# Unread f32 matmuls in TensorE's waits, and another split of the output projection, in a one-core decode kernel

## The chip, the cores and the metric

The kernel runs on one core of a Trainium2 chip. The metric is the device time of one execution in microseconds (us); the time of a kernel is the median of several executions. A profile is of one execution, and names the engines PE (TensorE matmuls), PEld (TensorE weight loads), DVE (VectorE), ACT (ScalarE), POOL (GpSimd) and SP (SyncE, which here only issues and awaits DMAs).

## What is computed

One decode step for two sequences (B = 2, one query each, D = 448), in bf16:

```python
xn = layernorm(A_x)                                  # 2 x 1 x 448
q  = (xn @ wq).reshape(B, 1, 16, 256)                # 16 query heads of 256
k, v = k_cache[:, :, -2048:], v_cache[:, :, -2048:]  # 8 key heads, each for two query heads
p  = softmax(q . k * 256**-0.5)
s  = (p . v).reshape(B, 1, 4096) @ wo                # wo: 4096 x 448
g  = silu(relu(xn @ w1) @ w2)                        # 448 -> 1792 -> 448
out = A_x + s * g
```

All matmuls have two tokens (or two tokens by two heads) of rows, so nearly all of the work is reading the caches and the weights once: 44.11 MB.

## The kernel before

**Loads.** All large loads are issued by SP in one queue, in program order: wq in two parts, K of turn 0, K of turn 1, V of turn 0, and later K and V of the following turns, w1 and w2 (L572, L573), V of the last turn (L588) and wo in pieces (L590 to L593). A turn is one quarter of the (sequence, key head) pairs; there are `NQ` = 4. K has two buffers, V one; wo goes into the first K buffer (L266). The next load of V waits for the PV that last read the buffer, the load of K for the DVE transposes that read it, and wo for the transposes of turn 2. SP takes its list in order, so each wait also holds what stands behind it.

**A turn.** DVE transposes K into `kt` (`do_T`, L455), PE makes the scores in `sbk` (`do_S`, L463, the two halves SA and SB), DVE takes the maxima, PE and DVE bring them to a bias (`ch_rmT`, `ch_mrow`, `ch_exp`), ACT takes the exponentials, DVE transposes them into `pt`. PE multiplies by V into `obk`, 32 matmuls on four column tiles (`do_PV`, L479); ACT scales the result to `o_sb` (L488); PE transposes that into `nbk` with four small matmuls (`do_oT`, L491, section OT), and DVE masks it into `at_exp` (`do_at`, L529).

**The order on PE.** PE's instructions are written into sections that `_Prog.run` (L115) lays out as a program with branches: SA, SB, PV, OT and CH are bodies that all turns share, with the turn in a register, so what stands in OT once runs in each of the four turns. The prologue (PRO), FFN, WO and END run once. PE takes its instructions in order, and each waits only for the operations named in its list of dependencies.

**The end.** With all turns but the last PV done, PE runs the FFN (`do_H`, `do_F`, L410 to L436), then PV, OT of the last turn. In WO two small matmuls fold `at_exp` (L609 to L612), DVE casts the result to `at2` (L613). wo has 32 rows per partition, of 448 columns each. The first `WO_WIDE` rows are "wide" (L615 to L619): one matmul of 448 columns a row, four rows side by side on the four column tiles of the array, row j on tile j % 4, summed into four places of `wbk`. DVE copies `wbk` to `wsum` (L620), and four f32 matmuls with `sel` add the four places into `cbk`, where the output's 448 columns lie as four tiles of 112 (L631 to L635). The rows left are "narrow" (`narrow`, L622): four matmuls of 112 columns a row, side by side, that add into the same places of `cbk`. Section END begins with the first row of the last piece of wo (L637). Then DVE multiplies by the gate and adds x (L640, L642), and ACT issues the DMA of the output.

wo comes in pieces of `WO_PARTS` rows (L194), each with a semaphore of its own; the first row of each piece waits for it. Before, these are 18, 8, 4 and 2 rows, with 26 wide ones (L195), so the wide rows end with the second piece.

`ident_f` is a 128 x 128 identity in f32 in SBUF. `sbk`, `obk`, `wbk`, `cbk` and so on are banks of PSUM, 128 x 512 in f32.

Of the kernel before, what the change touches and what calls it, by code (L numbers as in the profile page):

```python
# [11 lines left out]
PE, DVE, ACTE, SP, POOL = "pe", "dve", "act", "sp", "pool"  # L12
# [153 lines left out]
def bass_recurrent_scan__sliding_block_cached__dense_activation_relu__decode_kernel(  # L166
# [24 lines left out]
    SLOTS = 7  # L191
    HC = HD // 2
    FC = DFF // 2
    WO_PARTS = [18, 8, 4, 2]  # L194
    WO_WIDE = 26  # L195
    NCOL = D // 4
    QW = 24 + 8 * 128
    BIG = 1e30
# [2 lines left out]
    with es:  # L201
        pr = _Prog(nc, es)

        def named(name, shape, dt):
            return es.enter_context(nc.sbuf_tensor(name, shape, dt))

        def psum(name, shape, dt):
            return es.enter_context(nc.psum_tensor(name, shape, dt))

        def view(t, off, dims, n=128, p0=0, pstep=1):  # L210
            width = t.shape[1]
            return bass.AP(t, p0 * width + off, [[width * pstep, n]] + dims)

        ident = named("ident", [128, 128], BF)
        ident_f = named("ident_f", [128, 128], F32)
# [52 lines left out]
        sbk = psum("sbk", [128, 512], F32)  # L268
        obk = psum("obk", [128, 512], F32)
        fbk = psum("fbk", [128, 512], F32)  # L270
        wbk = psum("wbk", [128, 512], F32)
# [109 lines left out]
        def mm(out_ap, lhsT, rhs, start, stop=False, **kw):  # L381
            return lambda e: e.matmul(out_ap, lhsT=lhsT, rhs=rhs, start=start, stop=stop,  # L382
                                      skip_group_check=True, **kw)
# [95 lines left out]
        def do_PV(k):  # L479
            deps = [d_v[k], st["pt", k]]  # L480
            for n in range(NT // 2):
# [6 lines left out]
            st["osb", k] = pr.op(ACTE, lambda e: e.activation(  # L488
                o_sb[:, :], obk[:, :], ACT.Copy, scale=rs[:, k:k + 1]), [st["PV", k], st["rs", k]], key="osb")

        def do_oT(k):  # L491
            pr.section("OT", k + 1)
            deps = [st["osb", k]]
            for dhi in range(2):
                for t2 in range(2):
                    lo = 256 * t2 + 128 * dhi
                    o = pr.op(PE, mm(view(nbk, dhi, [[2, 8]]), o_sb[:, lo:lo + 128],
                                     fold[:, 8 * t2:8 * t2 + 8], dhi == 0 and t2 == 0, dhi == 1 and t2 == 1), deps)
                    deps = []
            st["oT", k] = o  # L500
# [57 lines left out]
        for k in range(1, NQ):  # L558
            if k > 1:
                ch_max(k)  # L560
            pr.section("PV", k)
            do_PV(k - 1)
            if k == 1:
                do_S(1, 1)
                ch_max(1)
            do_oT(k - 1)
            do_at(k - 1)
            load_v(k) if k < 3 else None
            if k == 1:
                load_k(3)  # L570
            if k == 2:
                d_w1 = pr.dma(SP, wbuf[:, 0:W2], w1_src, [st["q_mm"]])  # L572
                d_w2 = pr.dma(SP, wbuf[:, W2:W2 + 14 * D], w2_src)  # L573
            pr.section("CH", k)
            ch_rmT(k)
            ch_mrow(k)
            ch_exp(k)
            early = 2 if k == 1 else 0
            for e in range(early):
                do_T(k + 1, e)  # L580
            ch_pt(k)
            if k + 1 < NQ:
                do_qbd(k + 1)
                for e in range(early, 8):
                    do_T(k + 1, e)
                do_S(k + 1, 0)
                do_S(k + 1, 1)
        load_v(3)  # L588
        landed, j0 = {}, 0
        for n in WO_PARTS:  # L590
            landed[j0] = pr.dma(SP, wo_sb[:, j0 * D:(j0 + n) * D], wo_src[:, j0 * D:(j0 + n) * D],
# [10 lines left out]
        pr.section("PV", NQ)  # L602
        do_PV(NQ - 1)
        do_oT(NQ - 1)
        do_at(NQ - 1)

        pr.section("WO", 0)
        deps = [st["at", NQ - 1]]
        for b in range(2):  # L609
            m_at = pr.op(PE, mm(mbk[:, 256 + 32 * b:288 + 32 * b], at_exp[:, 128 * b:128 * b + 128],  # L610
                                fold[:, :], b == 0, b == 1), deps)
            deps = []  # L612
        v_at2 = pr.op(DVE, lambda e: e.tensor_copy(at2[:, :], mbk[:, 256:320]), [m_at])  # L613
        deps = [v_at2]
        for j in range(WO_WIDE):  # L615
            i = j % 4
            m_w = pr.op(PE, mm(wbk[32 * i:32 * i + 2, 0:D], view(at2, j, [[32, 2]]), wo_sb[:, j * D:(j + 1) * D],
                               j < 4, j + 4 >= WO_WIDE, tile_position=(0, 32 * i)), deps + [landed.get(j)])
            deps = []  # L619
        v_ws = pr.op(DVE, lambda e: e.tensor_copy(wsum[:, :], wbk[:, 0:D]), [m_w])  # L620

        def narrow(j):  # L622
# [9 lines left out]
        for i in range(4):  # L632
            pr.op(PE, mm(cbk[32 * i:32 * i + 17, 0:NCOL], sel[:, :], wsum[:, i * NCOL:(i + 1) * NCOL],
                         True, tile_position=(0, 32 * i)), deps)
            deps = []  # L635
        for j in range(WO_WIDE, 32):
            if j == max(landed):  # L637
# [39 lines left out]
```

## Time and profile before

| | |
|---|---|
| three executions, us | 110.31, 110.70, 110.76 |
| median | 110.7 us |
| the profiled execution's own time | 110.01 us |
| its span, first to last instruction | 108.7 us |
| mean granted TensorE clock in it | 0.874 |
| PE, DVE, ACT, POOL busy | 65.5, 62.2, 14.9, 7.9 us |
| DMA queue of the large loads | 44.11 MB, 95.1% of 16 engines' span |

The profile's times are microseconds from the span's start. A line of the timeline gives start, length, engine, line of the kernel, operation, written tile <- read tiles, shapes and count; the brackets hold the idle time of the engine before it and what ended it. Most matmuls have the line of a helper, L382, so they are told apart by their tiles. `kbuf` with `in_A_wo` as its source is wo, since wo lies in the first K buffer. `at` is `at2`. A row of the windows view gives a stretch, its length, busy us and instructions of PE, PEld, DVE, ACT and POOL, the granted TensorE clock (1.00 is full speed), the share of the DMA engines and GB/s. The chain that ended last is followed back from the last instruction, at each step to what released it.

### The profile page before, as it was taken

What the parts mean: (1) busy time and instruction counts of PE and PEld (TensorE: products, weight loads), DVE (VectorE), ACT (ScalarE), POOL (GpSimd) and SP (SyncE); (2) the same over time, 40 slices, a digit from 0 to 9 for tenths busy, and PEclk for the clock granted to TensorE, in tenths of its full rate; (3) what the DMA queues carried; (4) which work ended last, traced back from release to release, by engine and by line L of the source; (5) the groups of instructions that cost most, each with busy time, mean ns of one, the idle gap of its engine ahead of it and who ended that gap; (6) DMA issues with size and microseconds to landing.
All of it is one profiled execution on the core that took longest, in us unless ns stands there. A gap on an engine that the chain in (4) does not pass through costs nothing.

```text
span 108.7 us, 1107 instructions
## 1 busy us (share of the span) xinstructions
PE 65.5 (60%) x412; PEld 25.2 (23%) x412; DVE 62.2 (57%) x106; ACT 14.9 (14%) x33; POOL 7.9 (7%) x31
## 2 busy tenths in 40 slices
PE   0000930069973999942899954079994596675561
PEld 0000200023422333421334312024331331322210
DVE  1689078199948999043999413299932226214022
ACT  2991000000003001103000023000002300054000
POOL 6500023000021000030000210000000000000000
PEclk9999999999999759998559999557999556999769
DMA  3999998999899989998999889998999989999960
GB/s 72 457 423 448 458 458 386 434 446 470 386 422 410 519 386 422 398 531 386 398 422 531 386 386 434 458 458 386 404 415 402 539 386 422 410 435 392 417 239 1
DMA packets 2332, 44.11 MB, mean 406 GB/s; under 512 B 282, under 2 KB 412, under 8 KB 668
## 3 DMA queue, kind: packets, MB, share of 16 engines
q1 hardware_dynamic: 2304, 44.11, 95.1%
q10 hardware_dynamic: 28, 0.01, 0.0%
HBM read 44.11 MB, written 0.00 MB: 406 GB/s over the span
## 4 chain that ended last, share of the span: by engine, by line
DMA 61%; PE 20%; DVE 12%; SPq 2%; issue 1%; ACT 1%; DVEq 0%; ACTq 0%
DMA kbuf<-in_A_k_cache_dram 42%; DMA kbuf<-in_A_wo_dram 19%; PE sbk L382 14%; DVE kt L460 10%; PE obk L382 3%; SPq L46 2%; PE wbk L382 1%; ACT e_sb L521 1%; PE cbk L382 1%; DVE rm L503 1%; DVE wsum L620 1%; PE mbk L382 0%; PE nbk L382 0%; DVE mx L512 0%; DVE tmp L640 0%
## 5 line engine op out<-in xcount | busy, mean ns | idle before, releaser
L382 PE MATMUL sbk<-kt,qbd 128*128 128x512 bf16 x128 | 36.5, 449 | 13.1 <-DVE kt L460 13.0
L460 DVE STREAM_TRANSPOSE kt<-kbuf 128x1024 f32<-128x1024 f32 x32 | 36.7, 1206 | 7.2 <-DMA kbuf<-in_A_k_cache_dram 7.2
L382 PEld LDWEIGHTS sbk<-kt,qbd 128*128 128x128 bf16 x128 | 13.6, 110 | 35.3 <-issue 23.8
L382 PE MATMUL fbk<-wbuf,xq 128*4 128x512 bf16 x28 | 3.2, 627 | 10.9 <-DVE xq L369 10.9
L405 POOL COPY qbd<-qt 32x64 bf16<-32x64 bf16 x16 | 4.5, 284 | 54.1 <-PE sbk L382 42.2
L382 PE MATMUL obk<-vbuf,pt 128*16 128x512 bf16 x128 | 7.6, 379 | 0.8 <-DMA vbuf<-in_A_v_cache_dram 0.8
L488 ACT ACTIVATE o_sb<-obk,rs 128x512 bf16<-128x512 f32 x4 | 2.8, 688 | 37.7 <-PE obk L382 37.1
L503 DVE TENSOR_REDUCE rm<-sbk 128x1 f32<-128x512 f32 x4 | 2.8, 692 | 7.5 <-PE sbk L382 4.0
L520 ACT ACTIVATE bias<-mbk 128x1 f32<-128x1 f32 x4 | 0.7, 171 | 33.7 <-PE mbk L382 33.7
L526 DVE STREAM_TRANSPOSE pt<-e_sb 128x512 bf16<-128x512 bf16 x4 | 2.7, 687 | 3.2 <-ACT e_sb L521 3.2
L382 PE MATMUL nbk<-ssum,gsum 128*128 128x1 f32 x8 | 1.7, 286 | 4.5 <-ACT e_sb L521 4.5
L530 DVE TENSOR_TENSOR at_exp<-nbk,qmask 128x64 bf16<-128x64 f32 x4 | 0.9, 222 | 5.7 <-PE nbk L382 5.7
L382 PEld LDWEIGHTS obk<-vbuf,pt 128*16 128x16 bf16 x128 | 2.8, 89 | 5.3 <-DMA vbuf<-in_A_v_cache_dram 1.7
L382 PE MATMUL fbk<-wbuf,h_sb 128*17 128x448 bf16 x14 | 2.8, 352 | 2.0 <-DVE h_sb L426 2.0
L382 PE MATMUL wbk<-kbuf,at 128*2 128x448 bf16 x26 | 2.9, 565 | 1.5 <-DMA kbuf<-in_A_wo_dram 1.4
L382 PEld LDWEIGHTS fbk<-wbuf,xq 128*4 128x4 bf16 x28 | 0.8, 108 | 12.4 <-issue 11.8
L382 PE MATMUL mbk<-one_f,mrow 1*128 1x1 f32 x8 | 1.5, 256 | 2.8 <-DVE mrow L515 2.8
L620 DVE COPY wsum<-wbk 128x448 f32<-128x448 f32 x1 | 0.6, 624 | 4.2 <-PE wbk L382 4.2
L359 DVE TENSOR_SCALAR xg<-x_sb,st,rstd 2x384 bf16<-2x384 bf16 (+2 forms) x5 | 2.9, 601 | 0.1
L382 PE MATMUL cbk<-wbuf,xr 128*4 128x448 bf16 x7 | 2.8, 577 | 0.0
L521 ACT ACTIVATE e_sb<-sbk,bias 128x512 bf16<-128x512 f32 x4 | 2.7, 687 | 0.4
L382 PE MATMUL fbk<-wbuf,xr 128*4 128x448 bf16 x7 | 2.8, 571 | 0.0
(81 smaller groups left out, 43.7 us busy)
## 6 DMA issues: line engine op xcount, KB each, us to landing
kbuf<-in_A_k_cache_dram SPq DMA_DIRECT2D x4, 4096.0 KB, 23.1
vbuf<-in_A_v_cache_dram SPq DMA_DIRECT2D x4, 4096.0 KB
wbuf<-in_B_w_dram SPq DMA_DIRECT2D x2, 1568.0 KB, 20.8
wbuf<-in_A_wq_dram SPq DMA_DIRECT2D x1, 2560.0 KB, 10.4
kbuf<-in_A_wo_dram SPq DMA_DIRECT2D x1, 2016.0 KB, 19.0
wbuf<-in_A_wq_dram SPq DMA_DIRECT2D x1, 1024.0 KB, 4.8
kbuf<-in_A_wo_dram SPq DMA_DIRECT2D x1, 896.0 KB, 20.6
kbuf<-in_A_wo_dram SPq DMA_DIRECT2D x1, 448.0 KB, 21.3
```

The source lines that it names most:

```text
L46: o = _Op(eng, lambda e: e.dma_start(dst, src), deps, True, key)
L359: xs["xn"] = pr.op(DVE, lambda e: e.tensor_scalar(out=view(xg, 128 + 128 * lo + shift, [[256, blocks], [128, 2], [pairs, 128 // pairs]], n=B),
L382: return lambda e: e.matmul(out_ap, lhsT=lhsT, rhs=rhs, start=start, stop=stop, skip_group_check=True, **kw)
L405: st["qbd", k] = pr.op(POOL, lambda e, a=a: e.tensor_copy(view(qbd, 24 + 32 * a, [[128, 8], [2, 4], [1, 2]], n=32, p0=32 * a), view(qt, 0, ...
L460: st["T", k, e] = pr.op(DVE, lambda e: e.transpose(view(dst, lo, [[128, NT // 2], [1, 32]]), view(src, lo, [[128, NT // 2], [1, 32]])), de ...
L488: st["osb", k] = pr.op(ACTE, lambda e: e.activation(o_sb[:, :], obk[:, :], ACT.Copy, scale=rs[:, k:k + 1]), [st["PV", k], st["rs", k]], ke ...
L503: st["rm", k] = pr.op(DVE, lambda e: e.tensor_reduce(out=rm[:, :], in_=sbk[:, :], axis=AX.X, op=ALU.max), [st["S", k, 7]], key="rm")
L520: a = pr.op(ACTE, lambda e: e.activation(bias[:, :], mbk[:, 128:129], ACT.Copy), [o])
L521: st["exp", k] = pr.op(ACTE, lambda e: e.activation(e_sb[:, :], sbk[:, :], ACT.Exp, bias=bias[:, 0:1], accum_out=ssum[:, 0:1]), [a], key=" ...
L526: st["pt", k] = pr.op(DVE, lambda e: e.transpose(pt[:, :], e_sb[:, :]), [st["exp", k]], key="pt")
L530: st["at", k] = pr.op(DVE, lambda e: e.tensor_tensor(out=view(at_exp, 16 * k, [[64, 4], [4, 4], [1, 4]]), in0=view(nbk, 0, [[4, 4], [1, 4] ...
L620: v_ws = pr.op(DVE, lambda e: e.tensor_copy(wsum[:, :], wbk[:, 0:D]), [m_w])
```

## The change

wo's pieces become 18, 6, 6 and 2 rows, and 24 rows are wide instead of 26; the wide rows still end with the second piece, and six rows instead of four come between them and the last piece. A new helper puts a matmul on PE that multiplies the f32 identity by itself, repeated to n columns, into a bank that nobody reads at that time. It depends on nothing and nothing depends on it. It stands

- at the head of OT, ahead of the matmuls that wait for `o_sb`, in all four turns: 256 columns into `wbk`;
- in WO behind the two folding matmuls: 512 columns into `sbk`;
- behind wide row 17, the last of the first piece: 384 columns into `sbk`;
- behind the last wide row, 23: 256 columns into `sbk`.

```diff
-    WO_PARTS = [18, 8, 4, 2]
-    WO_WIDE = 26
+    WO_PARTS = [18, 6, 6, 2]
+    WO_WIDE = 24
...
+        def keep_busy(bank, n):
+            pr.op(PE, lambda e: e.matmul(bank[:, 0:n], lhsT=ident_f[:, :],
+                                         rhs=view(ident_f, 0, [[0, n // 128], [1, 128]]), start=True, stop=True))
+
         def do_oT(k):
             pr.section("OT", k + 1)
+            keep_busy(wbk, 256)
             deps = [st["osb", k]]
...
             deps = []
+        keep_busy(sbk, 512)
         v_at2 = pr.op(DVE, lambda e: e.tensor_copy(at2[:, :], mbk[:, 256:320]), [m_at])
         deps = [v_at2]
         for j in range(WO_WIDE):
...
             deps = []
+            if j == WO_PARTS[0] - 1:
+                keep_busy(sbk, 384)
+            if j == WO_WIDE - 1:
+                keep_busy(sbk, 256)
         v_ws = pr.op(DVE, lambda e: e.tensor_copy(wsum[:, :], wbk[:, 0:D]), [m_w])
```

## Prediction

> **What bounds the kernel now.** I read the page's slices and its chain first, then the DMA issues, then the chain in order of time, and last the end of the timeline beside the granted clock. The page:
>
> ```profile
> span 108.7 us, 1107 instructions
> ...
> DMA  3999998999899989998999889998999989999960
> ...
> HBM read 44.11 MB, written 0.00 MB: 406 GB/s over the span
> ...
> DMA 61%; PE 20%; DVE 12%; SPq 2%; issue 1%; ACT 1%; DVEq 0%; ACTq 0%
> ...
> kbuf<-in_A_wo_dram SPq DMA_DIRECT2D x1, 2016.0 KB, 19.0
> kbuf<-in_A_wo_dram SPq DMA_DIRECT2D x1, 896.0 KB, 20.6
> kbuf<-in_A_wo_dram SPq DMA_DIRECT2D x1, 448.0 KB, 21.3
> kbuf<-in_A_wo_dram SPq DMA_DIRECT2D x1, 224.0 KB, 21.4
> ```
>
> The DMA row is full from the second slice to the last but two: the kernel streams 44.11 MB, and nothing that TensorE does earlier moves the last byte as long as the queue keeps work. It does: the last V load, 4.19 MB, is issued at 82.14 and is landed when its PV starts at 96.98 (row below); at 406 GB/s it takes 10.3, so it began at 86.7 and had stood in line for some 4.5 us, with the wo pieces behind it. So only the end counts, behind the wo pieces. The chain in order of time, and the issues:
>
> ```profile
> 82.14 0.55 SPq L46
> ...
> 82.73 0.59 SPq L46
> ...
> 83.36 20.61 DMA kbuf<-in_A_wo_dram
> ...
> 104.02 0.95 PE wbk L382 x5
> ...
> 104.99 0.64 DVE wsum L620
> ...
> 105.66 0.70 PE cbk L382 x32
> ...
> 106.39 0.28 DVE tmp L640
> ...
> 106.70 0.28 DVE out_sb L642
> ```
>
> ```profile
> L46 SPq DMA_DIRECT2D kbuf<-in_A_wo_dram x4: 432/432/591, 82.7 to 84.3; - x4
> ```
>
> The pieces are issued at 82.73, 83.36, 83.83 and 84.31 (591 ns, then 432 ns each, about 0.04 between). With the page's times to landing they are there at 101.73, 103.97, 105.13 and 105.71. The chain follows the second piece: eight wide rows (0.95), the copy to wsum (0.64), then 8 sel and 24 narrow matmuls (0.70), and two VectorE operations. The last piece, at 105.71, lands just as sel starts at 105.66, so it isn't what ended last, but it is next in line.
>
> The clock comes from the windows view, cut where the grant changes. The changes lie on a grid of 3.41 us; the columns are length, PE busy, and further on PEclk:
>
> ```profile
> 81.31:84.72 3.41, 1.55 (x23) 0.65 (x15) 0.63 (x3) 0.88 (x3) 0.00 (x0) 1.00 0.99 416
> 84.72:88.13 3.41, 2.60 (x8) 1.22 (x9) 0.77 (x2) 0.76 (x2) 0.00 (x0) 0.50 1.23 525
> 88.13:91.55 3.42, 3.30 (x9) 0.89 (x7) 1.77 (x5) 0.00 (x0) 0.00 (x0) 0.50 0.93 402
> 91.55:94.96 3.41, 1.58 (x9) 0.82 (x10) 1.61 (x4) 0.00 (x0) 0.00 (x0) 1.00 0.94 404
> 94.96:98.37 3.41, 2.62 (x35) 1.08 (x37) 1.03 (x2) 2.02 (x8) 0.00 (x0) 1.00 1.01 432
> 98.37:101.78 3.41, 0.99 (x18) 0.29 (x10) 0.77 (x4) 0.69 (x1) 0.00 (x0) 1.00 0.91 385
> 101.78:105.20 3.42, 2.95 (x26) 0.66 (x26) 0.21 (x1) 0.00 (x0) 0.00 (x0) 0.50 0.94 373
> 105.20:108.61 3.41, 0.68 (x32) 0.52 (x32) 0.96 (x3) 0.00 (x0) 0.00 (x0) 1.00 0.00 1
> ```
>
> Each window's work sets the next window's clock. In 91.55:94.96, 1.58 us of long matmuls (46%) keep it at full; in 98.37:101.78, 0.99 (29%) halves it. The 1.55 of 81.31:84.72 halves it too, but half of that is short matmuls of 1 to 128 columns, mostly latency; its long ones, the PV of 80.19, end at 82.09, 0.78 us or 23%. So I count long ones, and the bound to hold full clock lies between about 29% and 46%. To come back, 61% (2.09 us of 84.72:88.13, from 86.04) was not enough and 86% was. The wide rows ran at half clock, and in this execution the grid was kind: the clock came back at 105.20, just ahead of sel.
>
> **The change part by part.** The rows that price it:
>
> ```profile
> 80.19 1.90 PE L382 MATMUL obk<-vbuf,pt 128*16 128x512 bf16 x32
> ...
> 86.04 2.77 PE L382 MATMUL fbk<-wbuf,xr 128*4 128x448 bf16 x7
> ...
> 88.61 2.82 PE L382 MATMUL cbk<-wbuf,xr 128*4 128x448 bf16 x7
> ...
> 93.38 2.81 PE L382 MATMUL fbk<-wbuf,h_sb 128*17 128x448 bf16 x14 [1.95 <-DVE h_sb L426]
> ...
> 96.98 1.90 PE L382 MATMUL obk<-vbuf,pt 128*16 128x512 bf16 x32 [0.79 <-DMA vbuf<-in_A_v_cache_dram]
> ...
> 98.99 0.69 ACT L488 ACTIVATE o_sb<-obk,rs 128x512 bf16<-128x512 f32 x1 [0.64 <-issue]
> 99.73 0.17 PEld L382 LDWEIGHTS nbk<-fold,o_sb 128*128 128x128 bf16 x4 [1.34 <-ACT o_sb L488]
> ...
> 100.31 0.21 PE L382 MATMUL mbk<-fold,at_exp 128*128 128x32 bf16 x2 [0.32 <-DVE at_exp L530]
> 100.56 0.23 DVE L613 CAST at<-mbk 128x64 bf16<-128x64 f32 x1 [0.31 <-PE mbk L382]
> ...
> 101.89 3.04 PE L382 MATMUL wbk<-kbuf,at 128*2 128x448 bf16 x26 [1.37 <-DMA kbuf<-in_A_wo_dram]
> ...
> 105.66 0.39 PE L382 MATMUL cbk<-wsum,sel 128*17 128x112 f32 x8 [0.73 <-DVE wsum L620]
> ...
> 105.87 0.48 PE L382 MATMUL cbk<-kbuf,at 128*17 128x112 bf16 x24
> ```
>
> ```profile
> 84.02 0.29 PEld L382 LDWEIGHTS mbk<-one_f,mrow 1*128 1x128 f32 x2 [0.89 <-DVE mrow L515]
> ...
> 85.53 0.50 PEld L382 LDWEIGHTS nbk<-ssum,gsum 128*128 128x128 f32 x2 [1.22 <-ACT e_sb L521]
> ```
>
> *One f32 filler.* No long f32 matmul stands in the trace. The four sel calls are eight instructions, so one f32 call is two. They occupy 105.66 to 105.87, 0.21 us for 112 columns on four tiles side by side. The 24 narrow bf16 matmuls, six rounds of 112 columns, take 0.48 less the last one's 0.21, so 0.045 a round. One f32 call thus costs about 0.21/0.045 = 4.6 bf16 rounds, latency included; I take 4, the count near it without latency. By the 14 rows of 93.38 (2.81 us, 0.19 a row of 448 columns) a bf16 column costs 0.42 ns at full clock; at half clock 0.82 (88.61 less 86.04 over 7 rows). Fillers of 256, 384 and 512 columns: 0.43, 0.64 and 0.86 us at full, about double at half clock; weights 0.29 at full, 0.50 at half, overlapped at best. Lower bound: as bf16, a quarter (0.11, 0.16, 0.21); upper: half clock with weights (1.3, 1.8, 2.2).
>
> *Fillers ahead of oT, one a turn.* PE waits there anyway: the last PV ends at 98.88 and oT waits for o_sb until 99.73. A 0.43 filler with 0.29 of weights ends by 99.6: nothing. At half clock (1.3) it would end at 100.2, 0.5 late. In earlier turns it could delay a later DMA issue by as much, against 4.5 us in line: nothing.
>
> *Filler of 512.* It starts at 100.52 and ends at about 101.7; the CAST runs beside it, and the first piece lands at 101.73: nothing, with no cover to spare. At half clock it ends at 102.7, and the first wide row is 0.9 late.
>
> *What the two do to the clock.* Window 98.37:101.78 holds 0.5 of PV, 0.43 and 0.86: 1.8 us, 52%, above the 46% that held. I expect 1.00 from 101.78. With the grid shifted, the poorest stretch, 98.9 to 102.3, has both fillers and 0.4 of wide rows, 50%.
>
> *Wide rows.* Four rows go side by side, so 18 rows are 4.5 rounds: 0.37 a round before, 0.19 now. They end their issue at 101.89 + 0.85 = 102.75 instead of 103.57. The 384 filler follows: 0.64 and some weights, to 103.5. Behind it in PE's queue are rows 18 to 23, then everything to the end. The second piece is now 672 KB: 896 took 103.97 - 101.73 = 2.24, so it takes 1.68 and lands at 103.41. Filler cost: 0.1. Rows 18 to 23 take 0.19 and 0.34 for the last (2.81 less 13 spacings of 0.19): 104.05. wsum 104.1 to 104.72 with the 256 filler beside it (103.9 to 104.6): nothing. sel at 104.75.
>
> *Narrow rows.* There are two more, 24 to 29 instead of 26 to 29, eight matmuls in two rounds, 0.09. Their 30 rows' bytes land at 105.13 as before. SP's issues, bytes and the last piece are unchanged. Rows 24 to 29 run by 105.5; the last two wait for 105.71, weights 0.10, two rounds 0.09, 0.21 for the last: 106.16.
>
> **The sum:** the end of PE's work goes from 106.37 to 106.16, 0.21 less, and the last landing is now the end's bound: no faster clock gains more here. The profiled execution had 110.01 (1.3 around its 108.7 span): 109.80.
>
> *Against the median.* 110.7 is 0.69 above that execution. I estimate where from: with the grid elsewhere, the old kernel's clock falls between 101 and 104.4 and returns only after 3.41 us of at least 61 to 86% work; a fall after about 102.2 leaves sel and narrow rows at half clock. That doubles 0.70 less 0.21, so +0.48, for some two thirds of the positions. The new kernel would not pay it. What is left, 0.21, stays. Forecast 110.01 - 0.21 + 0.21 = 110.0. Other end: all of 0.69 is something else, and 110.7 - 0.21 = 110.5. I take 110.1, nearer the first since the page's own row shows the clock returning only 0.46 us ahead of sel.
>
> The trace halved the clock at 101.78, behind a stretch from 98.88 to 101.89 in which PE still worked 0.5 us. The Trainium skill (TensorE: Matmul & The Clock Gate, section "HAM oscillation") only warns of gaps over about 3.4 us. By that rule these 3.0 us would cost no clock, the old tail would be at full clock and the fillers would earn nothing; the trace disagrees, with 0.50 granted. What it would give is the time of the second rival below, and I add nothing to that chance for it.
>
> **Rivals.**
>
> *Fillers don't count (slower).* An f32 matmul against an identity may not count as work, or half. Then 98.37:101.78 stays near 0.99, clock 0.50 from 101.78, and the fillers stand in line at double price. Rows 0 to 17 issue to 103.57, the 384 filler with weights to 105.1 or later, rows 18 to 23 to 106.05, wsum to 106.72, sel to the end 0.70 or, at half clock, 1.18: 107.4 to 107.9, that is 1.0 to 1.5 more than 106.37. With the 0.21: 111.2 to 111.7. It decides where 0.5 plus the counted part of 1.29 stays under the bound of 0.99 to 1.58 us: certainly below four tenths of their time, perhaps below eight. For it: no row shows a long f32 matmul. Against: f32 passes occupy the array for their length. The Trainium skill (TensorE: Matmul & The Clock Gate, Part 4, PE-mode transpose) says that transposes through TensorE do not count as busy in the same way; these fillers are plain matmuls, and no row here shows either.
>
> *The clock holds, but was not the loss.* The runs above 110.01 owe their time to DMA; then only 0.21 is gained: 110.3 to 110.7.
>
> *Partly held.* The clock falls in some grid positions; the 384 filler at half clock puts sel at about 105.7 and the end at 106.9, like the old kernel's usual end by my estimate: 110.5 to 110.8.
>
> *FFN drawn forward.* The 256 filler behind PV(2) may hold the clock at 84.72, H then ends sooner, PE idles before 96.98 for over 3.41 us, and the last PV runs at half clock. Window 81.31:84.72 gets 0.78 + 0.43, 35%, inside the open part of the bound. H at 0.19 instead of 0.37 a row saves 2.5 over its 14 rows; F waits for H; a PV of 1.90 at half clock takes 3.6: 111 to 111.7.
>
> **How the numbers follow.** Forecast (clock held, 109.7 to 110.3) 0.50; clock not the loss 0.22; partly held 0.14; fillers don't count 0.09; FFN drawn forward 0.05. A measurement tells about 0.5%, 0.55 us, from no change. Below 110.15 lie 0.42 of the forecast and 0.03 of the second case: faster 0.45. The last two cases are slower: 0.14. The rest, 0.41, is within. The range 109.6 to 110.8 holds the first three cases, 0.86; the slower two are left out.
>
> **What would show it.** Right: granted clock 1.00 from about 97 to the end; the 18 rows issued in under 1.1 us; wsum copied before the third piece lands; sel well ahead of 105.7; the chain ending on the last wo landing with eight narrow matmuls behind it. Wrong: 0.50 anywhere between 101 and 106; the wide rows 18 to 23 waiting for PE (the filler) rather than for DMA; oT or the first wide row late; wo landing later than 105.7.

## The result, and the profile after

The changed kernel takes 109.83 us (median of five executions, 109.69 to 109.95), against 110.7 before: a ratio of 0.9936, 95% interval 0.9907 to 0.9965, so faster by 0.3 to 0.9%: little, but clear of no change. The forecast was 110.1 us, and faster. The time around the span isn't constant (mostly 1.3 to 1.7 us, over 1.75 in some executions of most kernels), so below the span stands beside the time. The median span is 108.5 us after (108.4 to 108.6, five executions) and 109.2 before (108.4 to 110.0 in the 87 executions that ran beside the experiments below, 62 of them at 109.0 or more). The gain is largely that the long executions are gone.

The page of the changed kernel:

```profile
span 108.4 us, 1147 instructions
...
PEclk9999999999999959999558999556999755999999
DMA  2999998899899998999889988998899998899970
...
kbuf<-in_A_wo_dram SPq DMA_DIRECT2D x1, 2016.0 KB, 19.0
kbuf<-in_A_wo_dram SPq DMA_DIRECT2D x2, 672.0 KB, 20.7
...
kbuf<-in_A_wo_dram SPq DMA_DIRECT2D x1, 224.0 KB, 21.3
```

The DMA row is as full as before, and the pieces of wo take as long to land. PEclk ends in nines, where it ended 9769. The end of the timeline, PE's matmuls, and oT's weights (start, length, then idle time before in brackets):

```profile
98.86 0.70 PE L492 MATMUL wbk<-ident_f 128*128 128x256 f32 x2
...
99.77 0.17 PEld L382 LDWEIGHTS nbk<-fold,o_sb 128*128 128x128 bf16 x4 [0.61 <-ACT o_sb L488]
...
100.42 1.10 PE L492 MATMUL sbk<-ident_f 128*128 128x512 f32 x2
...
101.96 1.11 PE L382 MATMUL wbk<-kbuf,at 128*2 128x448 bf16 x18 [0.44 <-DMA kbuf<-in_A_wo_dram]
103.00 0.30 PEld L492 LDWEIGHTS sbk<-ident_f 128*128 128x128 f32 x2 [0.38 <-issue]
103.00 0.91 PE L492 MATMUL sbk<-ident_f 128*128 128x384 f32 x2
103.85 0.10 PEld L382 LDWEIGHTS wbk<-kbuf,at 128*2 128x2 bf16 x6 [0.55 <-DMA kbuf<-in_A_wo_dram]
103.85 0.54 PE L382 MATMUL wbk<-kbuf,at 128*2 128x448 bf16 x6
```

oT waits for `o_sb` still and starts at 99.77, as at 99.73 before. The first wide row waits for its DMA, not for the filler. Rows 18 to 23 stand behind the 384 filler, which the prediction had named as a sign of being wrong. The chain that ended last:

```profile
82.78 19.04 DMA kbuf<-in_A_wo_dram
...
101.96 1.11 PE wbk L382 x18
103.07 0.84 PE sbk L492 x2
103.92 0.49 PE wbk L382 x6
...
104.43 0.64 DVE wsum L630
...
105.11 0.94 PE cbk L382 x40
...
106.08 0.29 DVE tmp L650
```

It runs through the 384 filler, and not through the last landing as forecast. sel to the last narrow matmul is 105.11 to 106.05; before, PE ended at 106.37. The windows, cut on this execution's grid (the instants, 3.41 us apart, at which the granted clock can change):

```profile
95.47:98.88 3.41, 2.63 (x38) 0.91 (x35) 1.35 (x3) 2.02 (x8) 0.00 (x0) 1.00 0.88 374
98.88:102.30 3.42, 2.44 (x22) 1.02 (x22) 0.45 (x2) 0.69 (x1) 0.00 (x0) 1.00 0.92 385
102.30:105.71 3.41, 3.32 (x60) 1.39 (x48) 0.62 (x1) 0.00 (x0) 0.00 (x0) 1.00 0.79 316
```

Granted 1.00 over the whole end, where the kernel before had 0.50 from 101.78 to 105.20.

### The profile page after: what moved, and what is told of

It reads as the page before. It is cut to its first block, busy times and chain, and to the rows that moved or that the text cites. A ratio compares the mean times of both kernels' runs of the same rounds, so it can differ in the third digit from the quotient of the medians.

```text
span 108.4 us, 1147 instructions
## 1 busy us (share of the span) xinstructions
PE 69.6 (64%) x432; PEld 27.4 (25%) x432; DVE 62.2 (57%) x106; ACT 14.9 (14%) x33; POOL 7.9 (7%) x31
## 4 chain that ended last, share of the span: by engine, by line
DMA 60%; PE 29%; DVE 5%; SPq 2%; issue 1%; ACT 1%; DVEq 0%; ACTq 0%
DMA kbuf<-in_A_k_cache_dram 42%; PE sbk L382 22%; DMA kbuf<-in_A_wo_dram 18%; PE obk L382 3%; DVE kt L460 2%; SPq L46 2%; PE wbk L382 1%; PE cbk L382 1%; PE sbk L492 1%; ACT e_sb L526 1%; DVE rm L508 1%; DVE wsum L630 1%; PE mbk L382 0%; PE nbk L382 0%; DVE mx L517 0%
## 5 line engine op out<-in xcount | busy, mean ns | idle before, releaser
L382 PE MATMUL sbk<-kt,qbd 128*128 128x512 bf16 x128 | 37.0, 456 | 12.7 <-DVE kt L460 12.7
L492 PE MATMUL sbk<-ident_f 128*128 128x512 f32 (+2 forms) x6 | 2.7, 534 | 0.0
```

Source lines behind the costliest of these rows:

```text
L492: pr.op(PE, lambda e: e.matmul(bank[:, 0:n], lhsT=ident_f[:, :], rhs=view(ident_f, 0, [[0, n // 128], [1, 128]]), start=True, stop=True))
```

## Experiments

The theory: the fillers hold TensorE's clock over the gap behind the last PV, and the old kernel paid for the clock's fall in most executions. The rivals: the new pieces alone do it; fillers cost as much as they hold; DMA makes the spread. "Alone" means added to the kernel before, "without" means taken out of the changed one. Ratios are to the kernel before on the same chip.

**The kernel before once more** (no edit).

> The kernel before, for a second trace with the clock's grid elsewhere. Theory: the clock falls between 101 and 104.4 and, where it falls late, sel and the narrow rows run at half clock: 1.1 to 1.2 us instead of 0.70 from sel's start to the last narrow matmul, and the execution takes 110.3 to 110.8 us. Where the grid is as in the first trace: 0.70 and 110.0. Rival (DMA makes the spread): sel to the last narrow matmul takes 0.70 in either case and the last landing of wo comes later than 105.7.

It took 110.54 us, span 109.2. The last wide rows in its timeline, its chain from there, and its clock in the windows view:

```profile
104.09 0.91 PE L382 MATMUL wbk<-kbuf,at 128*2 128x448 bf16 x8 [1.00 <-DMA kbuf<-in_A_wo_dram]
```

```profile
105.05 0.64 DVE wsum L620
...
105.73 1.16 PE cbk L382 x32
```

```profile
103.00:104.00 1.00, 0.10 (x2) 0.00 (x0) 0.00 (x0) 0.00 (x0) 0.00 (x0) 1.00 0.96 387
104.00:105.00 1.00, 0.91 (x8) 0.10 (x8) 0.00 (x0) 0.00 (x0) 0.00 (x0) 0.57 1.00 385
105.00:106.00 1.00, 0.28 (x9) 0.26 (x12) 0.62 (x1) 0.00 (x0) 0.00 (x0) 0.50 0.13 45
```

Here the first 18 rows ran at full clock, the clock fell at 104.1, and sel with the narrow rows took 1.16 instead of 0.70: 0.46 more, forecast 0.48. The large loads end where they did, by about 105.2. The rival that DMA makes the spread falls for this execution.

**The pieces alone.**

```diff
-    WO_PARTS = [18, 8, 4, 2]
-    WO_WIDE = 26
+    WO_PARTS = [18, 6, 6, 2]
+    WO_WIDE = 24
```

> The new pieces of wo and 24 wide rows, no filler. Theory (the clock): the wide rows of most executions run at half clock as before; only the two wide rows fewer and the earlier second piece count, so the wide path is 0.2 to 0.4 us shorter and the time is 110.2 to 110.5 us, still with the spread of before, some 0.4 us between executions. Rival (the split does it all, the fillers are idle): 109.8 us, as the whole change.

110.13 us (109.75 to 111.28, 12 executions), ratio 0.997 (0.9938 to 1.0001); spans 108.4 to 108.9, median 108.5, none at 109. The chain of its profile, one of the longer spans (108.9):

```profile
102.03 2.48 PE wbk L382 x24
...
104.53 0.64 DVE wsum L620
...
105.21 1.34 PE cbk L382 x40
```

All 24 rows and then sel and the narrow rows ran at half clock (granted 0.52 from 101.83 to 105.24, 0.50 behind), and still PE ended at 106.55, 0.34 before the old kernel in the execution above. So the time is a little under what the theory forecast, and the long spans of the old kernel are gone without any filler, which it did not forecast. By the span's median the pieces alone reach the whole change, and 4 of 12 executions (108.8 and 108.9) are 0.3 to 0.4 us above it; by the time's median they gain 0.44 us (110.13 against 110.57), where the fillers alone, next below, gain 0.74; 3 of the 12 had over 1.75 us outside their span. What the pieces give lies between these two readings.

**The fillers alone**, in the old pieces (18, 8, 4, 2 rows, 26 wide).

> All fillers, but wo in pieces of 18, 8, 4, 2 rows and 26 wide. Theory: clock 1.00 through the end; the second piece lands at 104.0, its eight rows take 0.55, the copy 0.64, so sel starts at 105.25, and the last piece at 105.7 is the bound: end of PE's work at 106.1, the time 109.8 to 109.9 us, the whole gain. Rival (the split does it): 110.6 to 110.8 us.

109.83 us (109.72 to 111.35), ratio 0.9948 (0.9918 to 0.9978), as the theory had it; ten spans at 108.4 to 108.6, two at 108.9 and 109.0, median 108.45. Its chain:

```profile
104.08 0.58 PE wbk L382 x8
...
105.36 0.73 PE cbk L382 x32
```

0.58 and 0.73 at full clock; PE ends at 106.09. So by the spans each part alone gives most of the gain, and they don't add up.

**Without the late fillers.**

```diff
-            if j == WO_PARTS[0] - 1:
-                keep_busy(sbk, 384)
-            if j == WO_WIDE - 1:
-                keep_busy(sbk, 256)
```

> The split, the filler ahead of oT and the one of 512, but not the two of 384 and 256 between the wide rows and behind them. Theory: full clock at the wide rows in every execution; behind them PE idles, and in some positions of the grid the clock falls before sel, which adds up to 0.5 us there: 109.8 to 110.0 us in most executions, some at 110.2 to 110.3. Wide rows 18 to 23 start at their landing, 0.4 us sooner than behind the 384 filler, with no gain at the end, since the last piece lands at 105.7. Rival (all four fillers are needed): 110.3 us or more.

109.88 us (109.72 to 110.44), ratio 0.9947 (0.9923 to 0.997), spans 108.4 to 108.6 in all 12. The few falls expected before sel didn't show, neither in the spans nor in the trace. Its chain ends at the last piece:

```profile
85.29 20.65 DMA kbuf<-in_A_wo_dram
...
105.98 0.31 PE cbk L382 x8
```

Only the last two rows, eight matmuls, stand behind the last landing, and sel had started at 105.01. So here the landing is the bound, and the two late fillers buy nothing that is measured.

**Without the early fillers** (the pieces, 384 and 256 only), in twelve executions and then once more for a trace of the longer ones.

```diff
-            keep_busy(wbk, 256)
...
-        keep_busy(sbk, 512)
```

> The split and the two fillers of 384 and 256 columns behind wide rows 17 and 23, but none ahead of oT and no 512. The rival that forecast a loss, made on purpose: no filler holds the clock over the gap from 98.9 to 101.9 us. Theory: where the clock falls by 102, rows 0 to 17 issue to 103.6 and the 384 filler takes 1.3 to 1.5 us at half clock, so rows 18 to 23 start at about 105.1, not at their landing at 103.4, and PE ends at 107 or later: 110.7 to 111.5 us; where it falls later, the filler is half or not affected: 109.9 to 110.5. So a median of 110.2 to 110.9 and a spread of over 1 us. Rival (these fillers cost or gain nothing): 110.13 us, as with the split alone.

110.57 us (109.8 to 111.54), ratio 0.9996 (0.9953 to 1.0039). Spans fall in two groups: six at 108.5 to 108.8, six at 109.7 to 109.9.

> The two late fillers alone once more, for a trace of the slower group (6 of 12 had spans of 109.7 to 109.9 us). Theory: clock 0.50 at the wide rows, the 384 filler at half clock takes about 1.5 us, rows 18 to 23 start behind it at about 105.1 instead of at their landing, and PE ends at 107.3 to 107.9. Rival (a late DMA): rows 18 to 23 start at their landing, and that is late. In the faster group: span 108.5.

111.79 us, span 109.7, of the upper group:

```profile
102.06 1.19 PE L382 MATMUL wbk<-kbuf,at 128*2 128x448 bf16 x18 [1.02 <-DMA kbuf<-in_A_wo_dram]
103.18 1.65 PE L492 MATMUL sbk<-ident_f 128*128 128x384 f32 x2
104.75 0.91 PE L382 MATMUL wbk<-kbuf,at 128*2 128x448 bf16 x6
105.60 1.07 PE L492 MATMUL sbk<-ident_f 128*128 128x256 f32 x2
106.60 0.39 PE L382 MATMUL cbk<-wsum,sel 128*17 128x112 f32 x8
```

```profile
99.52:102.93 3.41, 1.34 (x24) 0.70 (x24) 0.76 (x4) 0.68 (x1) 0.00 (x0) 1.00 0.93 388
102.93:106.35 3.42, 3.42 (x16) 1.10 (x10) 0.62 (x1) 0.00 (x0) 0.00 (x0) 0.51 0.62 248
```

The clock fell at 102.93, just ahead of the 384 filler; the first 18 rows ran nearly all at full clock (1.19), where half clock was expected. The filler took 1.65 instead of 0.91, rows 18 to 23 went behind it at 104.75, and the 256 filler kept PE to 106.6. PE ended at 107.39, 1.3 later than in the change. This is the mechanism of the rival that forecast a loss, here from missing fillers rather than from fillers that don't count.

**Fillers of half the columns**, twelve executions and one more.

```diff
+            n = n // 2
             pr.op(PE, lambda e: e.matmul(bank[:, 0:n], lhsT=ident_f[:, :],
-                                         rhs=view(ident_f, 0, [[0, n // 128], [1, 128]]), start=True, stop=True))
+                                         rhs=view(ident_f, 0, [[0, n // 64], [1, 64]]), start=True, stop=True))
```

> The whole change with fillers of half the columns (128, 256, 192, 128). The first two bring 0.21 and 0.43 us into the stretch behind PV, where a window like 98.37 to 101.78 then has 0.5 + 0.64 = 1.14 us, 33%, in the part of the bound that the trace of before left open (29 to 46%). If the bound is near 46%: the clock falls there in nearly all positions, 110.1 to 110.3 us. If it is near 29%: held, 109.8 to 109.9 us. With a bound in between the executions differ by position.

110.6 us (109.71 to 111.57), ratio 0.9999 (0.996 to 1.0037), spans in two groups: five at 108.4 to 108.6, seven at 109.2 to 109.6.

> The halved fillers once more, for a trace of the slower group (7 of 12 executions had it). Theory: the clock falls between 101 and 104.4 us, rows and fillers behind the fall run at half clock, and wo lands as in the change; span 109.2 to 109.6. Rival (the slower group is a late DMA, as with the transposes): clock 1.00, and V or wo landing 0.7 us late or more. In the faster group: clock 1.00 and a span of 108.5.

110.7 us, span 109.4, of the upper group. Its windows, then its timeline:

```profile
98.34:101.75 3.41, 1.98 (x22) 0.86 (x14) 0.82 (x4) 0.73 (x2) 0.00 (x0) 1.00 0.92 386
101.75:105.16 3.41, 3.24 (x26) 1.15 (x26) 0.00 (x0) 0.00 (x0) 0.00 (x0) 0.51 0.96 387
```

```profile
101.92 2.03 PE L382 MATMUL wbk<-kbuf,at 128*2 128x448 bf16 x18 [0.86 <-DMA kbuf<-in_A_wo_dram]
103.88 1.01 PE L493 MATMUL sbk<-ident_f 128*128 128x192 f32 x2
104.82 0.71 PE L382 MATMUL wbk<-kbuf,at 128*2 128x448 bf16 x6
```

Counted by columns, as in the prediction, the first window holds 0.5 of PV, 0.21 and 0.43 of fillers: 33%, and the clock fell at its end. PE busy says 1.98, 58%, because it counts each matmul with its latency (0.49 and 0.68 for these two fillers, and the short ones besides); in the kernel before, a window with 1.58 busy (46%) kept the clock, so the busy column does not tell. wo lands as in the change; the theory holds, the late DMA doesn't. By the spans, fillers that are too small are worse than none (seven of 12 at 109.2 or more, against none of 12 with the pieces alone): they don't hold the clock in every position of the grid, and where it falls they stand in line at double price (1.01 for 192 columns).

**bf16 fillers of the same columns**, a quarter of the time.

```diff
-            pr.op(PE, lambda e: e.matmul(bank[:, 0:n], lhsT=ident_f[:, :],
-                                         rhs=view(ident_f, 0, [[0, n // 128], [1, 128]]), start=True, stop=True))
+            pr.op(PE, lambda e: e.matmul(bank[:, 0:n], lhsT=ident[:, :],
+                                         rhs=view(ident, 0, [[0, n // 128], [1, 128]]), start=True, stop=True))
```

> The whole change with fillers of the same columns in bf16 (the bf16 identity), so about a quarter of the time: 0.11 and 0.21 us behind PV, 0.8 us or 24% of such a window. Theory (TensorE's busy time holds the clock): it falls between 101 and 104.4 in nearly all positions, as without fillers, and the time is that of the split alone, 110.1 to 110.2 us. Rival (any instruction on PE in the gap is enough): 109.8 us.

110.3 us (109.74 to 111.4), ratio 0.9966 (0.9935 to 0.9997); spans 108.4 to 109.5, median 108.55. The time is that of the pieces alone or a little more, and the clock fell in its profile, at 103.66, with all four fillers in place. So the rival that any instruction will do falls, though by time and spans alone the difference to the whole change is small (eight of 12 spans are at 108.4 to 108.6). In that one trace wo also landed 0.7 us later than in the change. In the windows view from 105.4 to 105.9 its DMA share is 0.07, about one of 16 engines, where the change has 0.00, so one engine seems to have run late; no row says why, and it stays open.

**Without the filler ahead of oT.**

```diff
-            keep_busy(wbk, 256)
```

> The change without the filler ahead of oT, so behind PV only the 512 one. A window like 98.37 to 101.78 then has 0.5 + 0.86 = 1.36 us, 40%. The halved fillers (33%) gave two groups of executions, 108.4 to 108.6 and 109.2 to 109.6 us of span. If the bound to hold the clock lies at 40% or under: nearly all executions at 108.4 to 108.6, 109.8 to 109.9 us. If above: two groups again and a median of 110.2 or more.

110.15 us (109.68 to 111.26), ratio 0.9989 (0.9953 to 1.0026). Eight spans at 108.4 to 108.8, two at 108.9 and 109.0, two at 109.8 and 109.9: between the full and the halved fillers. So without the filler ahead of oT the clock seems to hold in most positions of the grid and not in all, and that filler is needed. The one trace is of an execution in which it held:

```profile
99.22:102.64 3.42, 2.01 (x24) 0.85 (x26) 0.45 (x2) 0.61 (x1) 0.00 (x0) 1.00 0.95 398
102.64:106.05 3.41, 3.32 (x60) 1.39 (x52) 0.62 (x1) 0.00 (x0) 0.00 (x0) 1.00 0.73 290
```

```profile
102.05 1.11 PE L382 MATMUL wbk<-kbuf,at 128*2 128x448 bf16 x18 [0.42 <-DMA kbuf<-in_A_wo_dram]
```

The first window holds the 512 filler, 0.86 by its columns, and 0.59 of the wide rows that begin at 102.05: 42%, and the next window has 1.00.

**Transposes as fillers**, all of them, and then only the early ones.

```diff
+            for i in range(n // 64):
+                lo = 128 * (i % (n // 128))
+                pr.op(PE, lambda e, lo=lo: e.matmul(bank[:, lo:lo + 128], lhsT=ident_f[:, :], rhs=ident_f[:, :],
+                                                    start=True, stop=True, is_transpose=True))
```

> The whole change with each filler made of transposes of the f32 identity through TensorE, 128 columns each, two per 128 columns of the filler: 4, 8, 6 and 4 instructions, each with its own f32 weights of 0.15 us, so 0.6 and 1.2 us of PE time behind PV by that estimate. If transposes count as work like matmuls: clock 1.00 to the end, 109.8 to 109.9 us. If they do not count, as the Trainium skill (TensorE: Matmul & The Clock Gate, Part 4, PE-mode transpose) has it: clock 0.50 at the wide rows in most executions, 110.1 us or more, and up to 111 where the later ones stand at half clock in front of rows 18 to 23.

111.12 us (110.98 to 111.69), ratio 1.0059 (1.003 to 1.0089): slower, by neither reason given. The clock stayed at 1.00 from 93.3 on. But the loads from the K of turn 2 on were 1.3 us late (DVE's transposes of it start at 51.91 instead of 50.65, and the last PV, waiting for V, at 98.30 instead of 97.03). The DMA view of its stretch from 30 to 40 us, and one row of the timeline:

```profile
q1 hardware_dynamic: 145, 4.19, 97.7%
q8 instruction: 1, 0.02, 0.7%
```

```profile
98.30 1.90 PE L382 MATMUL obk<-vbuf,pt 128*16 128x512 bf16 x32 [0.77 <-DMA vbuf<-in_A_v_cache_dram]
```

An instruction fetch of 16 KB lies in the stream of loads there; no other trace here has one of that size ahead of PE's last matmul.

The early ones alone, without the two late groups, as in the edit above that took the late fillers out:

> The split with f32 transposes ahead of oT (4) and behind the folding matmuls (8), and nothing between or behind the wide rows: ten instructions fewer than with all transposes. In the trace with all of them the clock stayed at 1.00, so transposes hold it, and yet the last V load landed 1.2 us late, with an instruction fetch of 16 KB in the trace at about 35 us. If the 1.2 us are that fetch and go with the length of PE's program: no such fetch here, wo lands as in the change, 109.8 to 109.9 us. If they belong to the transposes in the turns themselves: about 111 us again, with the late landing.

109.97 us (109.8 to 110.86), ratio 0.9966 (0.9937 to 0.9995), spans 108.3 to 108.5 in all 12, no such fetch. The transposes in the turns are the same, so the 1.3 us are not theirs; they come and go with the ten further instructions, and of the two traces the late one has the fetch. By the row above, the fetch took 0.7% of 16 engines' time over 10 us, 1.1 us if one engine carried it. And at the end of that trace, from 105.4 to 106.4, the DMA share is 0.06, about one of 16 engines, where the change has 0.00. That would fit one engine made late by the fetch and holding up each load's landing; it is argued from these figures, not shown by itself. The window of the kernel with the early ones alone shows what transposes do to the clock:

```profile
100.35:103.77 3.42, 2.74 (x38) 1.55 (x38) 0.45 (x2) 0.07 (x1) 0.00 (x0) 1.00 0.97 401
103.77:107.18 3.41, 1.38 (x46) 0.55 (x40) 1.17 (x3) 0.00 (x0) 0.00 (x0) 0.98 0.37 145
```

Besides the eight transposes, the first window has only the 24 wide rows, 1.1 us or 33%, the share at which the halved fillers lost the clock. It held, so f32 transposes, with their weight loads, count. The Trainium skill (TensorE: Matmul & The Clock Gate, Part 4, PE-mode transpose), on which one of the expectations drew, says that transposes do not count as busy in the same way; as far as keeping the full clock goes, this run disagrees.

## Why the prediction was right, point by point

- **The bound.** Nearly right. DMA and its end didn't move, and only the tail changed. The last landing was to be the bound at the end. In the kernel without late fillers it is (0.31 us of PE behind it); in the changed kernel the chain runs through the 384 filler and PE's matmuls instead, and ends at 106.05. A landing at 105.7 plus that 0.31 gives 106.0, so the two paths end almost together.
- **A filler's price.** Right: 0.70, 0.91 and 1.10 us for 256, 384 and 512 columns, forecast 0.43, 0.64 and 0.86 plus weights of 0.29. Each further 128 columns cost 0.20, so 1.6 ns a column, 3.7 times the 0.42 of bf16.
- **Early fillers at nothing.** Right: oT at 99.77, the first wide row waits for its landing.
- **The clock held.** Right: 1.00 to the end. The bound that I left between 29 and 46% is now between 33% (fell, the halved fillers) and about 42% (held, without the filler ahead of oT), each read in one trace. By my own count of long matmuls the lower end was 23%, not 29%: of the 0.99 in 98.37:101.78 only 0.5 is PV, and the rest is short matmuls. The 86% that I gave for the clock's return is 89% by the spacing of the rows; nothing rests on it.
- **Wide rows and the 384 filler.** Mis-sized. Forecast: rows 18 to 23 start at 103.5, 0.1 after landing, sel at 104.75. Measured: 103.85 and 105.11. The f32 weights start only at 103.00, behind an idle 0.38, and the filler ends 0.4 after the landing forecast for 103.41. So a sign of being wrong showed, rows waiting for the filler, but it cost nothing measurable at the end: without the late fillers, 109.88.
- **The sum in the profiled execution.** Forecast 0.21, measured 0.31 (109.70 against 110.01; PE's end 106.05 against 106.37). The terms of the forecast for PE's end (105.71, 0.10, 0.09 and 0.21) add up to 106.11 and not to the 106.16 given, so to 0.26.
- **Against the median.** The forecast median was 0.60 below the old one, the measured one is 0.87 below: the sum gave 0.1 more than forecast, and the part that I let stay, 0.21, is 0.13 here (109.83 against 109.70). The half clock behind a late fall was right in mechanism and size (0.46 for 0.48). What I gave wrongly is whose saving it is: "The new kernel would not pay it" credits the fillers alone. The pieces alone also take out a good part of it, since they bring sel forward from 105.73 to 105.21, even at half clock, into time that the wait for the last piece covers. I used the smaller piece's earlier landing in the sum and priced the split's two further narrow rows at 0.09, but didn't ask what the pieces would save without fillers.
- **The rivals.** "Fillers don't count" fell, but its price was right: fillers at half clock in front of rows cost 1.3 at PE's end, forecast 1.0 to 1.5. "The clock was not the loss" fell too: in the second trace of before, the clock and not DMA made the longer span. "Partly held" didn't appear in the change, but it describes the halved fillers and the kernel without the filler ahead of oT. "FFN drawn forward" didn't appear in the change. In other traces the second part of the FFN ran at half clock, the second one of before among them; there oT came at 100.69 instead of 99.73, still ahead of wo.

## What to carry to other kernels

Where a tail follows a stream of loads, look first for what can be moved ahead of the last landing: here a split that did so, and fillers that made the same work faster, each gave most of the gain as the spans have it, and together hardly more than one. A filler must be big enough to hold the clock and must end before the wait in which it stands is over; one that is too small, or that stands ahead of real work when the clock has already fallen, is worse than none. And a median can hide two groups of executions: the one profiled first was of the lucky kind, and only the spread told that the typical one is longer, by 0.46 us of half clock in the second trace.

## What the runs showed of the hardware

- TensorE's granted clock changed on a grid of 3.41 us (in the first trace of before at 84.72, 91.55, 101.78 and 105.20), at another offset in other executions (102.93 and 103.66 in two of them). Full clock was kept after a window with about 42% of its time in long matmuls or fillers (without the filler ahead of oT) and lost after windows with 25% (0.87 of wide rows, without the early fillers) and 33% (halved fillers). The PE busy column is no measure of it: 58% of busy lost it (1.98 of 3.41 us, halved fillers), 46% kept it (1.58, the kernel before).
- f32 transposes through TensorE held the clock in a window with otherwise some 33% of its time in long matmuls, and all 12 spans of that kernel are at 108.3 to 108.5.
- The kernel with the most TensorE instructions had spans of 109.6 or more in all 12 executions; its trace has a 16 KB instruction fetch amid the loads, and loads 1.3 us late from there on. That the one causes the other is argued.
